# A delta-rule attention and two MoEs on one core: x^T of the first tile completed in PSUM, and the second MoE's second layer turned round

## The chip, the core and the metric

The kernel runs on one core of a Trainium2 chip. Its engines each have a queue of their own: TensorE (PE, with its weight loads as PEld), VectorE (DVE), ScalarE (ACT), GpSimd (POOL) and SyncE (SP, which here only issues DMAs). The metric is the device time of one execution in microseconds. Three runs of the kernel before took 1483.88, 1479.08 and 1480.54 us, median 1480.54. The profiled execution is another run.

## The reference

All inputs are float32 but for the first MoE's weights, which come in as 64-bit floats and are made float32 on the chip. Three stages follow each other:

```
attention, 4 batches x 8 heads, 768 steps, head size 48:
    k = k / (|k| + 1e-6)
    y[t] = q[t] . state                       # the state before this step
    state += beta[t] * k[t] (v[t] - k[t] . state)
x = y, heads side by side                     # 3072 tokens x 384
first MoE:   h = x @ w_in (384 x 2048);  x = (h * sigmoid(1.702 h)) @ w_out
second MoE:  p = domain_probs / (sum over 4 experts + 1e-9)
             out = sum over e of p[:, e] * (relu(x @ w1[e] (384 x 1024)) @ w2[e])
```

## The kernel before

**Units and tiles.** The 768 steps are cut into 12 units of 64 steps, for all batches and heads at once. Two units are one tile of 512 tokens (128 for each of the four batches), so there are 6 tiles. In a unit the recurrence is solved by blocks: a gram of the keys (`gp`, L511 and L514), the inverse of a triangular matrix (`queue_first_inverse` for units 0 and 1, on DVE with two groups of products on PE, L661 and L670; `queue_inverse` for later pairs, on POOL), a gram of queries with keys that DVE masks (the q gram, L444, L449), and then the chain (`queue_chain`): `ks`, `solve`, `cross`, `solve` again (L733, L743, L753), `read` (y, L765), `write` (L770) and the addition to the state `SU` (L784, L787). A chain is done for two halves of the heads, `hu` 0 and 1; in units 0 and 1 one half after the other.

**The way from y to x^T.** `read` leaves y in the PSUM bank with the tag `yg`, 48 rows for even heads at 0 and for odd heads at 64. `y_copy` (L773) puts three of each four heads into the tile `stage` and the fourth into another buffer; six DMAs for a unit (`put`, L848; in units 0 and 1 three on SP and three on ACT's queue) bring the fourth heads, 16 rows at a time, under the others, so that `stage` holds x^T with 128 rows in each of three blocks. Then `split_x` (L876) splits it into two float32r parts, a high one (a cast) and a low one (a subtraction, L878). Each product in the MoEs is three matmuls: high x high, high x low, low x high (`PASSES`).

**The MoEs.** For each of 16 blocks of 128 hidden columns (8 blocks in each expert of the second MoE) a visit has a first layer, 9 matmuls into `ph` (L884), and the second layer of the block before, so that the gate on ACT and DVE has a visit's time. In the first MoE the second layer has the weights stationary and 512 tokens moving, 9 matmuls into `px` (L972), and leaves x^T again. In the second MoE it has the hidden values `hh` stationary, 128 tokens at a time, and the weights moving, 12 matmuls of 384 columns into four banks `po` (L1086); rows are tokens then, and DVE multiplies by p as a scalar of each row (L1092, L1094). Each of the four experts goes over the six tiles. In tile 0 of the first MoE the first 8 blocks are done for unit 0's 256 columns, then for unit 1's, then the last 8 for 512 columns; tile 1 is done in halves throughout (`HALVED`).

**The order.** Each engine works through its own queue in the order in which the program issues. Attention and the preparation of the weights (`queue_w1`: loads, three steps that make float32 of 64-bit values, a high cast L274 and a low subtraction L277) are tasks of the planner `Order`: each has an engine or two to choose from, a cost, a priority, what it depends on, and `can`, a function that tells from when a buffer is free or None. Between the MoE's matmuls `tick` issues what is ready by the planner's clock; `until` issues tasks until the ones named are done by that clock. Before the first matmul of the first MoE stands `until(ydone[0], wdone[0])`, then one for the split.

**The second MoE's buffers.** Its weights come through `raw`, two halves of 768 columns, and are split by ACT and DVE (`split_w2`, L229 and L230); those of the next expert during the last tile. x of tiles 0 to 3 goes out to DRAM and comes back at the end of tile 4. `split_now` (L1074) splits a tile's x; that of the first tile stands behind the first MoE's end. When the first MoE ends its PSUM pools are closed (`ph` banks 0 and 1, `px` 2 to 4, the attention's `yg`, `ch0`, `ch1` 5 to 7), and the second MoE's pool takes the banks anew.

Of the kernel before, what the change touches and what calls it, by code (L numbers as in the profile page):

```python
# [149 lines left out]
def delta_attention_moe_moe_kernel(  # L150
# [17 lines left out]
    E = probs.shape[1]  # L168
    F2 = we.shape[0] // E
# [52 lines left out]

    def load_w2(n):
        nc.sync.dma_start(out=raw[:, n % 2, :], in_=we[n])

    def split_w2(n):
        t = wp.tile([128, 2, 768], F32R, name="w", tag="w")
        half = raw[:, n % 2, :]
# [94 lines left out]
    V = nc.vector  # L323

# [98 lines left out]
    def queue_q(u):  # L423
# [11 lines left out]
        for g0 in range(0, NP, 8):  # L435
# [251 lines left out]
    def queue_chain(u):  # L687
# [27 lines left out]
        for hu in range(2):  # L715
# [65 lines left out]
            def s_add(x, gs=gs, cell=cell):  # L781
# [4 lines left out]
                else:  # L786
# [3 lines left out]
                               read=read, write=write, y_copy=y_copy, s_add=s_add))  # L790


        for hs in [halves[0:1], halves[1:2]] if u < 2 else [halves]:
# [29 lines left out]
            if n == 1:  # L823
                h, = hs
                reads = [task(h["read"], "PE", 1.0, (*bs, pdone[u]), prio=p, can=lambda: free_at("yg"))]
# [4 lines left out]
            for h, y in zip(hs, reads):  # L830
                ye = h["cell"]["yev"] = [task(lambda e, x=x, h=h: h["y_copy"](e, x), ("ACT", "DVE"), (0.7, 0.72), (y,), prio=p,
                                              can=y_free) for x in range(2)]
                wr = task(h["write"], "PE", 0.82, bs, prio=p) if n == 1 else reads[0]
# [7 lines left out]


        ov = []
        for x in range(2):
            for kk in range(KD):
                def put(x=x, kk=kk):
                    d, n = DR[x] + 16 * kk, DR[x] + D
                    (nc.scalar if u < 2 and x else nc.sync).dma_start(out=xst[n:n + 16, kk, u % 2], in_=YS[u][d:d + 16])  # L848

                ov.append(task(put, "ACT" if u < 2 and x else "HW", 0.45, yev, lat=2.3, prio=p, slack=5))  # L850
# [5 lines left out]
    xst = stage.rearrange("p (k c b i) -> p k c b i", k=KD, b=B, c=2)  # L856

# [31 lines left out]
    with tc.manual_schedule():  # L889
# [6 lines left out]
        nc.gpsimd.memset(SU, 0.0)  # L896
        m2 = scr[2][:, 0:C]
# [33 lines left out]
        x1 = {}  # L931
        x1d = [drx.tile([128, KD, TT], F32, name=f"x1d{t}") for t in range(KEEP)]
# [4 lines left out]
        def queue_w2(n):  # L937
            e, f = divmod(n, F2)
            WE[e, f] = split_w2(n)
            if n + 2 < E * F2:  # L940
                load_w2(n + 2)

        def x1_out(t):
# [16 lines left out]
            return ev  # L960

# [44 lines left out]
        def split_stage(t, cs, us, fs):  # L1006
            if not us:
                return split
            until(*(ydone[u] for u in us))
            if cs.start == 0:  # L1010
# [173 lines left out]
```

## Time and profile before

| | |
|---|---|
| runs, median (lowest, highest) | 1480.54 us (1479.08, 1483.88) |
| the profiled execution | 1484.33 us |
| its span, from first to last instruction | 1482.6 us |
| mean granted TensorE clock | 0.974 of full speed |
| PE busy | 1420.4 us, 96% |
| DVE, ACT, POOL busy | 619.3, 459.8, 191.9 us |
| matmuls ph, po, px | 2808, 2304, 1080 |

The page cuts the span into 40 slices of 37 us. PE's busy tenths are 3, 6, 8, 7 in the first four and 9 from the fifth on; the granted clock is 8, 5, 8, 8 tenths in the first four and 9 or more behind them. Busy time is a union of records, and matmuls are pipelined: what a matmul costs is read from the distance of starts, not from its own duration. In the rows below the first column is the start in us from the span's start, the second the time from the first start to the last end of a merged row; a bracket at the end tells how long the engine was idle before and what ended that.

### The profile page before, as it was taken

How to read it: one execution, taken by the hardware profiler on the slowest of the kernel's cores; microseconds unless marked ns; L12 is line 12 of the kernel's file. 1: busy time of each engine (PE TensorE's matmuls, PEld its weight loads, DVE VectorE, ACT ScalarE, POOL GpSimd, SP SyncE). 2: the span in 40 equal slices, each digit the busy share in tenths (PEclk: the TensorE clock that was granted, in tenths of full speed). 3: DMA queues.
4: the chain of work that ended last, by engine and by line, in shares of the span. 5: the costliest groups of instructions: out<-in, count | busy, mean ns of one | idle time of the engine just before them, and what ended most of it. 6: DMA issues, size and time to landing. Idle time of an engine off the chain costs nothing.

```text
span 1482.6 us, 30388 instructions
## 1 busy us (share of the span) xinstructions
PE 1420.4 (96%) x13552; PEld 1258.2 (85%) x13552; DVE 619.3 (42%) x1033; ACT 459.8 (31%) x866; POOL 191.9 (13%) x340
## 2 busy tenths in 40 slices
PE   3687999999999999999999999999999999999999
PEld 2677889998888788888999999999999999999998
DVE  6978756545473423332223242232433223423222
ACT  5554434445353233432111231121321112222111
POOL 2019550080260530000000000000000000000000
PEclk8588999999999999999999999999999999999999
DMA  9211021201201000410000020000200000100001
GB/s 316 115 27 36 2 74 34 62 22 26 49 23 37 15 33 8 142 52 1 0 1 0 10 77 0 1 0 1 64 22 0 1 0 22 43 22 22 22 22 43
DMA packets 41331, 53.71 MB, mean 36 GB/s; under 512 B 25712, under 2 KB 29936, under 8 KB 41200
## 3 DMA queue, kind: packets, MB, share of 16 engines
q1 hardware_dynamic: 41008, 51.67, 11.7%
q8 instruction: 106, 1.74, 0.5%
q14 instruction: 25, 0.20, 0.0%
q10 hardware_dynamic: 192, 0.10, 0.0%
HBM read 42.71 MB, written 7.86 MB: 34 GB/s over the span
## 4 chain that ended last, share of the span: by engine, by line
PE 90%; DVE 2%; DMA 1%; ACT 1%; SPq 0%; issue 0%; DVEq 0%
PE ph L884 40%; PE po L1086 27%; PE px L972 13%; PE ch L743 2%; PE gp L444 2%; PE ch L733 1%; PE y L765 1%; DMA pq<-in_q_dram 1%; PE ch L753 1%; PE ch L770 1%; PE gp L511 1%; SPq L848 0%; DVE w L277 0%; DVE gh L990 0%; DVE scr L479 0%
## 5 line engine op out<-in xcount | busy, mean ns | idle before, releaser
L884 PE MATMUL ph<-xs,w 128*128 128x512 f32 (+1 forms) x2808 | 664.8, 379 | 3.7 <-DVE x L180 2.4
L884 PEld LDWEIGHTS ph<-xs,w 128*128 128x128 f32 x2808 | 499.7, 190 | 90.3 <-issue 2.8
L1086 PE MATMUL po<-w,hh 128*128 128x384 f32 x2304 | 432.8, 336 | 0.0
L1086 PEld LDWEIGHTS po<-w,hh 128*128 128x128 f32 x2304 | 407.6, 188 | 17.1
L1113 DVE SCALAR_TENSOR_TENSOR hh<-ph,hh 128x512 fp32r<-128x512 f32 x192 | 132.9, 692 | 554.0 <-ACT hh L1112 554.0
L1112 ACT ACTIVATE hh<-ph 128x512 fp32r<-128x512 f32 x192 | 115.0, 599 | 632.3 <-PE ph L884 632.3
L972 PE MATMUL px<-gh,w 128*128 128x512 f32 (+1 forms) x1080 | 233.5, 356 | 0.6 <-DVE gh L990 0.4
L972 PEld LDWEIGHTS px<-gh,w 128*128 128x128 f32 x1080 | 178.5, 192 | 29.4 <-DVE gh L990 2.0
L990 DVE TENSOR_TENSOR gh<-ph,gh 128x512 fp32r<-128x512 f32 (+1 forms) x120 | 69.5, 579 | 147.7 <-ACT gh L989 146.9
L987 ACT ACTIVATE ph<-ph 128x512 f32<-128x512 f32 (+1 forms) x120 | 59.5, 496 | 207.8 <-PE ph L884 203.5
L569 POOL TENSOR_TENSOR scr<-scr,itmp 128x30 f32<-128x30 f32 (+9 forms) x150 | 89.4, 596 | 11.8
L567 POOL TENSOR_TENSOR itmp<-scr 128x30 f32<-128x30 f32 (+9 forms) x150 | 81.4, 543 | 11.4
L989 ACT CAST gh<-ph 128x512 fp32r<-128x512 f32 (+1 forms) x120 | 60.2, 502 | 3.8
L180 ACT COPY su<-ch 32x384 f32<-32x384 f32 x77 | 36.2, 471 | 49.6 <-PE ch L743 45.0
L444 PE MATMUL gp<-pq,kt 48*64 48x64 f32 x768 | 34.2, 254 | 18.1 <-DMA pq<-in_q_dram 9.5
L444 PEld LDWEIGHTS gp<-pq,kt 48*64 48x64 f32 x768 | 31.3, 166 | 21.4 <-issue 8.3
L1078 DVE TENSOR_TENSOR xs<-x,xs 128x512 fp32r<-128x512 f32 x72 | 45.3, 684 | 2.0 <-ACT xs L1077 2.0
L511 PE MATMUL gp<-kt 48*32 48x64 f32 x768 | 28.2, 231 | 17.0 <-ACT kt L180 16.2
L743 PEld LDWEIGHTS ch<-v,scr 32*32 32x32 f32 x1536 | 36.5, 110 | 7.8 <-issue 4.6
L511 PEld LDWEIGHTS gp<-kt 48*32 48x32 f32 x768 | 25.2, 116 | 20.8 <-ACT kt L180 17.6
L743 PE MATMUL ch<-v,scr 32*32 32x48 f32 x1536 | 40.4, 208 | 0.7 <-DVE pq L449 0.5
L180 ACT COPY kt<-scr 32x512 f32<-32x512 f32 (+1 forms) x60 | 37.0, 617 | 12.0 <-DVE scr L333 11.1
(106 smaller groups left out, 809.6 us busy)
## 6 DMA issues: line engine op xcount, KB each, us to landing
raw<-in_we_dram SPq DMA_DIRECT2D x32, 384.0 KB, 3.1
rw<-in_w_dram SPq DMA_DIRECT2D x14, 768.0 KB, 12.2
k<-in_k_dram SPq DMA_DIRECT2D x12, 384.0 KB, 5.1
pq<-in_q_dram SPq DMA_DIRECT2D x24, 192.0 KB, 4.5
v<-in_v_dram SPq DMA_DIRECT2D x12, 384.0 KB, 3.2
out_dram<-oacc SPq DMA_DIRECT2D x24, 192.0 KB, 1.9
x1d<-raw SPq DMA_DIRECT2D x12, 256.0 KB, 2.3
x<-x1d SPq DMA_DIRECT2D x4, 768.0 KB, 5.8
```

The source lines that it names most:

```text
L180: (nc.scalar.copy if e == "ACT" else nc.vector.tensor_copy)(out=out_, in_=in_)
L444: mm(ps[TR[x]:TR[x] + C, i, :], lhsT=kt[d:d + D, g, :], rhs=pq[d:d + D, g, x, :], start=True, stop=True)
L511: mm(ps[r:r + SB, i, :], lhsT=kt[d:d + D, g, 0:SB], rhs=kt[d:d + D, g, :], start=True, stop=True)
L567: E.tensor_tensor(out=tv, in0=x[:, j:j + 1, j + 1:].broadcast_to([128, m, r]), in1=x[:, 0:m, j:j + 1].broadcast_to([128, m, r]), op=ALU.mult)
L569: E.tensor_tensor(out=x[:, 0:m, j + 1:], in0=x[:, 0:m, j + 1:], in1=tv, op=ALU.add)
L743: mm(cell["ps"][r:r + 32, i, :], lhsT=Tb[u][r:r + 32, g, :], rhs=V2[u][r:r + 32, g, :], start=True, stop=True, tile_position=(r, r))
L884: mm(ps, lhsT=w[:, a, kk * 128:(kk + 1) * 128], rhs=xs[kk][:, b, cs], start=kk == 0 and i == 0, stop=kk == KD - 1 and i == 2)
L972: mm(px[d][:, cs], lhsT=w[:, a, 384 + d * 128:384 + (d + 1) * 128], rhs=gh[:, b, 0:cs.stop - cs.start], start=f == 0 and i == 0 and cs.sta ...
L990: a = task(lambda: nc.vector.tensor_tensor(out=lo, in0=ph, in1=hi.bitcast(F32), op=ALU.subtract), "DVE", 0.07 + 0.53 * c, (a,), **kw)
L1086: mm(po[b], lhsT=hh[:, a, b * 128:(b + 1) * 128], rhs=w[:, c, 384:768], start=f == 0 and i == 0, stop=f == F2 - 1 and i == 2)
L1112: nc.scalar.activation(out=hh[:, 0, :], in_=ph, func=AF.Relu)
L1113: nc.vector.scalar_tensor_tensor(out=hh[:, 1, :], in0=ph, scalar=0.0, in1=hh[:, 0, :].bitcast(F32), op0=ALU.max, op1=ALU.subtract)
```

## The change

**x^T of the first tile.** For units 0 and 1 the rows of the fourth heads are no longer moved by DMA. A tile `S4`, which lies in `stage`'s memory and is set to zero at the start, takes from the state the columns of the fourth heads, 16 for each of three blocks, behind 48 columns of zeros (`fourth`). For each head of the first three in four, `read` now does two matmuls: one with `S4` (64 columns stationary) and the fourth head's queries, one with the head's own state on top of it. The bank then holds x^T with 64 rows in each half, and `take_x` and `take_rest` split it straight from PSUM into `xs0`. `stage`, the DMAs and `split_x` stay for the other tiles. A `can` keeps q grams of units over 1 out until the first MoE runs, and `write` in the first units now comes behind `read`.

**The second MoE.** For tiles 0 to 4 the second layer has the weights stationary and `hh` moving, 9 matmuls of 512 columns into three banks; the result has d_model in rows, so p is loaded as a row that stands in all 128 partitions (`load_pb`, into `raw`'s second half, from the DRAM tile `prd`), DVE multiplies (the first expert straight into the sum, the others in the bank and then an addition), and after the last expert DVE transposes 32x32 blocks and 16 DMAs a tile write the output. Tile 5 keeps the old form (`layer2_last`). The weights of w2 are laid out with their columns permuted to fit. The pool of `po` is opened first (banks 0 to 5), that of `ph2` second (6 and 7). The first tile's split stands at block 12 of the first MoE's last tile. The next expert's weights are split two in each of tiles 1 to 4 through `raw`'s first half.

On PE, around the first tile's first matmul (`ph`): `y` is `read`, `ch<-su,k` is `write`, `gp<-scr` the inverse's two products for unit 1, `gp<-kt_76` unit 2's gram, `gp<-pq_78,kt_76` unit 2's q gram. Before:

```order
L765 MATMUL y<-pq_78,su 48x64 x16
L770 MATMUL ch_652<-su,k_0_81 48x48 x16
L770 MATMUL ch_675<-su,k_0_81 48x48 x16
L661 MATMUL gp<-scr_100,scr_99 32x16 x64
L670 MATMUL gp<-scr_98,scr_100 32x16 x64
L765 MATMUL y<-pq_78,su 48x64 x16
...
L444 MATMUL gp<-pq_78,kt_76 64x64 x32
L884 MATMUL ph<-xs,w 128x256 x18
```

After, where `stage` is the name of `S4`'s memory:

```order
L776 MATMUL y<-pq_78,stage 64x64
L777 MATMUL y<-pq_78,su 48x64
L799 MATMUL ch_679<-su,k_0_81 48x48 x16
...
L521 MATMUL gp<-kt_76 32x32 x2
L931 MATMUL ph<-xs,w 128x256 x18
L518 MATMUL gp<-kt_76 32x64 x2
```

The inverse's products, the q gram and half of the gram have moved behind the first 18 `ph`.

On DVE, from the same place: `rw` and `w` are steps on the weights of the first MoE, `su<-ch` the state's first values, `kt` keys, `scr<-gmask,bt` the premask of units 2 and 3. Before, x^T is split (L878) 18 rows behind the last of these:

```order
L269 SCALAR_TENSOR_TENSOR rw<-rw 128x768
L787 COPY su<-ch_652 48x8x48 x2
L265 TENSOR_SCALAR rw<-rw 128x768
L269 SCALAR_TENSOR_TENSOR rw<-rw 128x768
L180 COPY kt_76<-scr_101 16x16x32
L265 TENSOR_SCALAR rw<-rw 128x768
L479 TENSOR_TENSOR scr_101<-gmask,bt 128x1024
```

After:

```order
L273 SCALAR_TENSOR_TENSOR rw<-rw 128x768
L269 TENSOR_SCALAR rw<-rw 128x768
L793 TENSOR_TENSOR xs<-y,xs 128x128 x3
L816 COPY su<-ch_656 48x8x48 x2
L273 SCALAR_TENSOR_TENSOR rw<-rw 128x768
L181 COPY kt_76<-scr_101 16x16x32
L269 TENSOR_SCALAR rw<-rw 128x768
L486 TENSOR_TENSOR scr_101<-gmask,bt 128x1024
L793 TENSOR_TENSOR xs<-y,xs 128x128 x3
L816 COPY su<-ch_679 48x8x48 x2
```

The rows are the same ones, with the state's copy (L787, now L816) two rows later; the six subtractions (L793) stand among them.

On DVE at the end of a tile in the last expert, where `hh` is the low half of the next block. Before:

```order
L1113 SCALAR_TENSOR_TENSOR hh<-ph_10295,hh 128x512
L1094 SCALAR_TENSOR_TENSOR oacc<-po,pr,oacc 128x384 x4
L1113 SCALAR_TENSOR_TENSOR hh<-ph_10324,hh 128x512
```

After:

```order
L1218 SCALAR_TENSOR_TENSOR hh<-ph_12836,hh 128x512
L1165 TENSOR_TENSOR po<-po,raw 128x512
L1166 TENSOR_TENSOR oacc_7904<-oacc_7904,po 128x16x32
L1165 TENSOR_TENSOR po<-po,raw 128x512
L1166 TENSOR_TENSOR oacc_7904<-oacc_7904,po 128x16x32
L1165 TENSOR_TENSOR po<-po,raw 128x512
L1166 TENSOR_TENSOR oacc_7904<-oacc_7904,po 128x16x32
L1171 STREAM_TRANSPOSE oacc_7904<-oacc_7904 128x768 x2
L1218 SCALAR_TENSOR_TENSOR hh<-ph_12882,hh 128x512
```

Eight operations stand between two `hh` where four stood. The diff, cut to its core:

```diff
+    xs0 = [xsp.tile([128, 2, TT], F32R, name="xs", tag="xs") for _ in range(KD)]
...
-                         (*placed[u], lq, begun[0], *ends[-1:]), prio=p + 1, can=lambda: some_free(BANKS, whole))
+                         (*placed[u], lq, begun[0], *ends[-1:]), prio=p + 1,
+                         can=lambda: None if u > 1 and not od.moe else some_free(BANKS, whole))
...
                     o, c0 = DR[x], (g * 2 + x) * D
-                    mm(py[o:o + D, i, :], lhsT=SU[:, c0:c0 + D], rhs=pq[:, g, x, :], start=True, stop=True)
+                    if not t and g % 4 == KD:
+                        continue
+                    if not t:
+                        g3 = g - g % 4 + KD
+                        mm(py[o:o + C, i, :], lhsT=S4[:, g // 4, x, g % 4, :], rhs=pq[:, g3, x, :], start=True, stop=False)
+                    mm(py[o:o + D, i, :], lhsT=SU[:, c0:c0 + D], rhs=pq[:, g, x, :], start=bool(t), stop=True)
+
+            def fourth(e, hu=hu):
+                bs = slice(hu * B // 2, (hu + 1) * B // 2)
+                copy(e, S4[:, bs, :, :, D:].rearrange("p b x k i -> p (b x k) i"),
+                     SU[:, 0:NP * 2 * D].rearrange("p (b m y) -> p b m y", b=B, m=4)[:, bs, KD, :])
+
+            def take_x(e, kk, hu=hu, cell=cell):
+                c0 = (u % 2) * TT // 2 + hu * TT // 4
+                copy(e, xs0[kk][:, 0, c0:c0 + TT // 4].rearrange("p (b i) -> p b i", i=C),
+                     cell["py"].rearrange("p (b m) i -> p m b i", m=4)[:, kk])
...
+                bs.append(task(h["fourth"], ("ACT", "DVE"), (0.35, 0.35), bs, prio=p))
+                reads = [task(h["read"], "PE", 1.5, (*bs, pdone[u]), prio=p, can=lambda: free_at("yg"))]
...
+                    for kk in range(KD):
+                        a = task(lambda e, kk=kk, h=h: h["take_x"](e, kk), ("ACT", "DVE"), (0.3, 0.27), (y,), prio=-2)
+                        ye += [a, task(lambda kk=kk, h=h: h["take_rest"](kk), "DVE", 0.28, (a,), prio=-2)]
...
+        if not t:
+            direct[u] = yev
+            ydone[u] = task(lambda: None, None, 0.0, yev, lat=0.0, prio=p)
+            return
...
+    S4 = stage.rearrange("p (b x k i) -> p b x k i", b=B, x=2, k=KD)
...
         nc.gpsimd.memset(SU, 0.0)
+        nc.gpsimd.memset(stage, 0.0)
...
+                if t == NW - 1 and f == F1 - 4:
+                    first = [split_now(0, 0, kk) for kk in range(KD)]
...
+        pso = ctx.enter_context(tc.tile_pool(name="pso", bufs=6, space=PSUM))
         ps2 = ctx.enter_context(tc.tile_pool(name="ps2", bufs=2, space=PSUM))
...
+            pb[e, t] = raw[:, 1, 0:TT]
+            nc.sync.dma_start(out=pb[e, t], in_=prd[e:e + 1, t * TT:(t + 1) * TT].broadcast_to([128, TT]))
...
         def layer2_2(e, t, f, hh, w):
+            acc = oacc[t].rearrange("p (c k j) -> p k c j", k=KD, j=32)
+            for kk in range(KD):
+                if f == 0:
+                    po[kk] = pso.tile([128, TT], F32, name="po", tag="po")
+                for i, (a, c) in enumerate(PASSES):
+                    mm(po[kk], lhsT=w[:, a, 384 + kk * 128:384 + (kk + 1) * 128], rhs=hh[:, c, :],
+                       start=f == 0 and i == 0, stop=f == F2 - 1 and i == 2)
+                if f == F2 - 1:
+                    ps = po[kk]
+                    if e == 0:
+                        nc.vector.tensor_tensor(out=acc[:, kk], in0=ps.rearrange("p (c j) -> p c j", j=32),
+                                                in1=pb[e, t].rearrange("p (c j) -> p c j", j=32), op=ALU.mult)
+                        continue
+                    nc.vector.tensor_tensor(out=ps, in0=ps, in1=pb[e, t], op=ALU.mult)
+                    nc.vector.tensor_tensor(out=acc[:, kk], in0=acc[:, kk], in1=ps.rearrange("p (c j) -> p c j", j=32),
+                                            op=ALU.add)
+            if f == F2 - 1 and e == E - 1:
+                for h in range(2):
+                    half = oacc[t][:, h * KD * TT // 2:(h + 1) * KD * TT // 2]
+                    nc.vector.transpose(out=half, in_=half)
...
+                if e + 1 < E and 1 <= t <= F2 // 2 and f in (2, 4):
+                    queue_w2((e + 1) * F2 + (t - 1) * 2 + f // 2 - 1)
...
-        layer2_2(*pend)
+        (layer2_last if pend[1] == NW - 1 else layer2_2)(*pend)
```

## Rows read from the trace of the kernel before

**Rows 1.** The page: busy us, share of the span and instructions of each engine.

```profile
PE 1420.4 (96%) x13552; PEld 1258.2 (85%) x13552; DVE 619.3 (42%) x1033; ACT 459.8 (31%) x866; POOL 191.9 (13%) x340
```

**Rows 2.** Timeline of PE from 66 to 91 us: start, us, line, what.

```profile
66.61 1.54 PE L661 MATMUL gp<-scr,scr 32*32 32x16 f32 x128 [1.61 <-DVE su L787]
69.87 1.90 PE L670 MATMUL gp<-scr,scr 32*32 32x16 f32 x128 [1.71 <-ACT scr L180]
71.70 1.95 PE L765 MATMUL y<-pq,su 128*48 128x64 f32 x32
...
82.94 3.67 PE L444 MATMUL gp<-pq,kt 48*64 48x64 f32 x62 [0.86 <-DMA pq<-in_q_dram]
86.55 4.21 PE L884 MATMUL ph<-xs,w 128*128 128x256 f32 x18
```

**Rows 3.** Windows, 25 to 75 us: length, then each engine's busy time, clock, DMA.

```profile
25.00:75.00 50.00, 30.77 (x1059) 28.52 (x1058) 43.61 (x90) 28.03 (x45) 0.00 (x0) 0.56 0.47 186
```

**Rows 4.** Timeline of PE from 118 to 154 us.

```profile
118.56 1.10 PE L765 MATMUL y<-pq,su 128*48 128x64 f32 x32
...
131.55 2.29 PE L884 MATMUL ph<-xs,w 128*128 128x256 f32 x9
...
151.75 2.23 PE L884 MATMUL ph<-xs,w 128*128 128x512 f32 x9
```

**Rows 5.** Timeline of DVE from 61 to 83 us.

```profile
61.08 1.82 DVE L417 TENSOR_TENSOR k<-k,scr 128x768 f32<-128x768 f32 x2
...
63.30 1.30 DVE L333 STREAM_TRANSPOSE scr<-k 128x512 f32<-128x512 f32 x2
...
68.99 1.22 DVE L479 TENSOR_TENSOR scr<-gmask,bt 128x1024 f32<-128x1024 f32 x1
...
82.45 0.42 DVE L878 TENSOR_TENSOR xs<-stage,xs 128x256 fp32r<-128x256 f32 x1 [0.46 <-ACT xs L180]
```

**Rows 6.** Timeline of DVE from 130 to 133 us.

```profile
130.65 1.00 DVE L265 TENSOR_SCALAR rw<-rw 128x768 int32<-128x768 int32 x1
131.69 1.25 DVE L269 SCALAR_TENSOR_TENSOR rw<-rw 128x768 int32<-128x768 int32 x1
```

**Rows 7.** Timeline of PE from 189 to 206 us.

```profile
189.46 1.64 PE L770 MATMUL ch<-su,k 64*48 64x48 f32 x64
...
193.76 1.10 PE L765 MATMUL y<-pq,su 128*48 128x64 f32 x32
...
197.28 2.07 PE L733 MATMUL ch<-su,kt 48*64 48x48 f32 x64
...
205.17 1.34 PE L884 MATMUL ph<-xs,w 128*128 128x256 f32 x9
```

**Rows 8.** Timeline of PE from 640 to 680 us, end of the first MoE.

```profile
641.01 2.20 PE L972 MATMUL px<-gh,w 128*128 128x512 f32 x9
...
669.57 4.29 PE L972 MATMUL px<-gh,w 128*128 128x512 f32 x18
676.30 4.36 PE L884 MATMUL ph<-xs,w 128*128 128x512 f32 x18 [2.43 <-DVE x L180]
```

**Rows 9.** The chain that ended last, in the second MoE: start, us, what.

```profile
684.85 2.10 PE po L1086 x12
...
1370.39 2.10 PE po L1086 x12
```

**Rows 10.** Timeline of DVE from 911 to 917 us, at a tile's end.

```profile
911.28 0.69 DVE L1113 SCALAR_TENSOR_TENSOR hh<-ph,hh 128x512 fp32r<-128x512 f32 x1 [3.50 <-ACT hh L1112]
...
915.46 0.69 DVE L1113 SCALAR_TENSOR_TENSOR hh<-ph,hh 128x512 fp32r<-128x512 f32 x1 [1.38 <-ACT hh L1112]
```

**Rows 11.** Timeline of PE at the same tile's end.

```profile
918.80 2.24 PE L1086 MATMUL po<-w,hh 128*128 128x384 f32 x12
```

**Rows 12.** Timeline of POOL, inverse of units 2 and 3.

```profile
104.55 0.16 POOL L561 MEMSET scr<- 128x32 f32 x1 [94.20 <-PE ph L884]
...
153.83 1.92 POOL L573 TENSOR_TENSOR scr<-scr,bt 128x1024 f32<-128x1024 f32 x1
```

More of the change, by code (lines that the diff above doesn't have):

```diff
@@ L789, in queue_chain @@
             halves.append(dict(hu=hu, cell=cell, ks=ks, rest=rest, solve=solve, solved=solved, cross=cross, rest2=rest2,
-                               read=read, write=write, y_copy=y_copy, s_add=s_add))
+                               read=read, write=write, y_copy=y_copy, s_add=s_add, fourth=fourth,
+                               take_x=take_x, take_rest=take_rest))
         for hs in [halves[0:1], halves[1:2]] if u < 2 else [halves]:
@@ L830, in queue_chain @@
             for h, y in zip(hs, reads):
-                ye = h["cell"]["yev"] = [task(lambda e, x=x, h=h: h["y_copy"](e, x), ("ACT", "DVE"), (0.7, 0.72), (y,), prio=p,
-                                              can=y_free) for x in range(2)]
-                wr = task(h["write"], "PE", 0.82, bs, prio=p) if n == 1 else reads[0]
+                if t:
+                    ye = [task(lambda e, x=x, h=h: h["y_copy"](e, x), ("ACT", "DVE"), (0.7, 0.72), (y,), prio=p,
+                               can=y_free) for x in range(2)]
+                else:
+                    ye = []
+                    for kk in range(KD):
+                        a = task(lambda e, kk=kk, h=h: h["take_x"](e, kk), ("ACT", "DVE"), (0.3, 0.27), (y,), prio=-2)
+                        ye += [a, task(lambda kk=kk, h=h: h["take_rest"](kk), "DVE", 0.28, (a,), prio=-2)]
+                    xfree.setdefault((0, 0), []).append(y)
+                    xfree.setdefault((0, 1), []).append(y)
+                h["cell"]["yev"] = ye
+                wr = task(h["write"], "PE", 0.82, (y,), prio=p) if n == 1 else reads[0]
                 se = [task(lambda x=x, h=h: h["s_add"](x), "DVE", 0.47, (wr, y), prio=p) for x in range(2)]
@@ L847, in put @@
                     d, n = DR[x] + 16 * kk, DR[x] + D
-                    (nc.scalar if u < 2 and x else nc.sync).dma_start(out=xst[n:n + 16, kk, u % 2], in_=YS[u][d:d + 16])
-                ov.append(task(put, "ACT" if u < 2 and x else "HW", 0.45, yev, lat=2.3, prio=p, slack=5))
+                    nc.sync.dma_start(out=xst[n:n + 16, kk, u % 2], in_=YS[u][d:d + 16])
+                ov.append(task(put, "HW", 0.45, yev, lat=2.3, prio=p, slack=5))
         whole["end"] = ov
@@ L960, in x1_out, with split_now @@
             return ev
+        def split_now(n, t, kk):
+            s = (xsp if n % 2 else xs2).tile([128, 2, TT], F32R, name="xs", tag="xs")
+            src = x1[t][:, kk, :]
+            nc.scalar.copy(out=s[:, 0, :], in_=src)
+            nc.vector.tensor_tensor(out=s[:, 1, :], in0=src, in1=s[:, 0, :].bitcast(F32), op=ALU.subtract)
+            return s
         evac = []
@@ L1009, in split_stage @@
             until(*(ydone[u] for u in us))
+            if not t:
+                xs[:] = xs0
+                return [a for u in us for a in direct[u]]
             if cs.start == 0:
@@ L1064, in delta_attention_moe_moe_kernel @@
                 load_w2(1)
[L1065 removed]
+                nc.sync.dma_start(out=pr, in_=probs)
         layer2_1(*pend)
@@ L1097, in layer2_2 @@
                         r0 = b * S + t * 128
-                        nc.sync.dma_start(out=out[r0:r0 + 128, :], in_=acc)
+                        nc.sync.dma_start(out=out[r0:r0 + 128, :], in_=acc[:, b])
         pend = None
         seq = [(e, t) for e in range(E) for t in range(NW)]
-        xs = [split_now(0, 0, kk) for kk in range(KD)]
+        load_pb(0)
+        pr5 = big.tile([128, E, B], F32, name="pr5")
+        for e in range(E):
+            nc.sync.dma_start(out=pr5[:, e], in_=prd[e, (NW - 1) * TT:].rearrange("(b p) -> p b", b=B))
+        xs = first
         for n, (e, t) in enumerate(seq):
```

81 lines of the change are left out of this document (51 added, 30 removed).

## The prediction

> **What bounds the kernel now.** I read the page first. PE is busy for 96% of the span [rows 1], so only two things can move the time: stretches in which PE does not work or works slowly, and the time that a matmul takes where PE never stops. The page's slices of PE and of its clock put the first kind into the first tenth of the span and show the second everywhere behind it. So I read three stretches in the timeline: the start up to the first tile's first matmul, the pure stretch of the first MoE beside the second MoE, and the seam between them.
>
> At the start PE waits for x^T of unit 0. Its second half of y is done at 71.70 + 1.95 = 73.65 us, but the first ph comes at 86.55 [rows 2]. In between stand the DMAs that bring the fourth heads into `stage`, the split, and 64 matmuls for unit 2's q (the last 62 take 3.67 us) which the planner put there because it thought PE free. DVE sets the pace before: it is busy for 43.6 of the 50 us from 25 to 75 [rows 3]. The same picture comes back for unit 1: y is done at 118.56 + 1.10 = 119.66, and ph goes on at 131.55 [rows 4], with a group of q matmuls between.
>
> **First tile, unit 0.** Until 61.08 us DVE's order is the same row for row. From there to the premask (the 128x1024 product with gmask) it keeps the same twelve instructions, which took from 61.08 to 68.99 + 1.22 = 70.21, 9.1 us without a gap [rows 5]; six subtractions of 128x128 now stand among and behind them. One of 128x256 takes 0.42, so these cost between 0.2 and 0.42; I take 0.3. So x^T of unit 0 is ready at 61.08 + 9.1 + 1.8 = 72.0, where PE started on it at 86.55. What ACT and PE add lies beside DVE: the copy of the fourth heads, three casts a half, 24 matmuls a half for 16. The second half's y must wait until the first half has left the bank `yg`: that lies within the walk, since five rows of DVE stand between the two groups of subtractions.
>
> **Unit 1.** What is moved behind the first ph is unit 1's two inverse products (1.54 and 1.90, [rows 2]), half a gram of unit 2 (about 1) and unit 2's q matmuls, all on a PE that until then idled. Before, PE went without a gap from 86.55 to 119.66, 33.1 us. Now this stretch takes 33.1 + 3.4 + 1 + 2 (the q matmuls at the higher clock, about half of 3.67) + 1.1 (half as many y matmuls again) = 40.6, from 72 to 112.6; with the last casts and subtractions unit 1's x^T is there at 114. DVE, walked in the same way through the W blocks, comes out at 114 too: the two are level, and I expect small waits on both. Before, it was 131.55: some 17 us are won here.
>
> **The pass over unit 1** ran from 131.55 to 151.75, 20.2 us [rows 4]. Now DVE has more left to do in it: three more W blocks want their tensor_scalar and their shift, 1.00 and 1.25 while POOL works beside [rows 6], 6.8 us together, of which its gaps take some; unit 3's q matmuls lie in it too, about 2. I take 23: the first 512-wide ph at 137 instead of 151.75, 14 us won.
>
> **The seam to tile 1** gives some back. Unit 2's x^T still goes through `stage` and the DMAs, and in the new order nothing but attention stands between unit 2's y and tile 1's first ph. From the second y's end to that ph it took 205.17 - 194.86 = 10.3 us [rows 7], some 8 of it chain; with two reads of 1.1 and a copy of about 1 between them the chain from the first y is 11.3 us, in which PE has two reads 2.2, the write 1.64, ks 2.07 and a solve of some 1.5, 7.5 us of work. So 3.8 us idle, which were none. Left: 10.5 us. Behind it PE is full to 673 us in either order but for single microseconds, so a start that is earlier by so much ends earlier by as much. Bounds: 3 us (a seam of 8, W blocks late as well) and 17 (nothing given back).
>
> **Costed at nothing.** The memset of `stage` on POOL moves PQ[1]'s and with it q's second load and all behind it on SP, by one memset (between 1 and 2 us by its size). DVE's own chain of the first inverse, up to 40 us, hides that; without the cover it is those 1 to 2 us. Six DMAs on SP instead of three there and three on ACT matter for no tile: the first two units now issue none, and from tile 1 on all six were SP's already.
>
> **Seam of the MoEs.** Before, PE is idle for 2.43 us up to 676.30, released by DVE's last copy of px [rows 8]. Now the first split is made four blocks earlier, and the first two ph2 lie in banks 6 and 7, whose last users were the chains, long done; px's banks are wanted two ph2 later, 4 us. So 2.5 us go (bounds 0 and 2.6, the gap that a stream without a stop would leave).
>
> **Second MoE, second layer turned.** A visit is 9 matmuls of 512 columns for the first layer and, for five of six tiles, now 9 of 512 instead of 12 of 384: 4608 columns both ways. So the price of a matmul beyond its columns decides. Before: from the po at 684.85 to the one at 1370.39 there are 164 visits, 4.180 us each [rows 9]. The first MoE's pure stretch has the new form already (the weights stationary in both layers, 512 columns): from 641.01 to 669.57 stand seven visits, 4.080 us each [rows 8]. The difference, 0.100 us by 160 visits, is 16.0 us. The bound on the other side is the ph group of the second MoE itself: 4.18 - 2.10 = 2.08 where the first MoE has 2.04. Were the turned group to take 2.08 too, 3 us would be won; if it kept 2.10, nothing. I take 16, because the first MoE has both shapes and the unevenness can come only from the mixture of 512 and 384, which goes away.
>
> The Trainium skill speaks against this: its page "TensorE: Matmul & The Clock Gate", section "Back-to-back issue gap", gives N / 2.4 + 2.5 ns for one matmul behind another at the full clock. By that page 9 x 215.8 stand against 12 x 162.5 ns, 8 ns a visit, and turning the layer round would win 1 us in all. The trace disagrees with it: 126 matmuls of 512 in 28.56 us are 226.7 ns each [rows 8].
>
> On DVE each tile's end costs more: a multiplication in the bank and an addition for each of three blocks from the second expert on, six of 512 for four of 384; in the last expert two transposes of 128x768 more (128x512 takes 0.65 to 0.70 in [rows 5], so about 1.0 each). Queued behind them is the next block's hh. Before, one hh starts at 911.28 and the next at 915.46, and the second lasts to 916.15 [rows 10], so 3.5 us lie between; six operations at hh's 0.69 take 4.1, with transposes 6.1. PE reads that hh in the po group at 918.80 [rows 11], 2.7 us later, so a delay of 0.6 or 2.6 is just covered. If it isn't, the five transposing tiles lose up to 1 us each. The split of the weights, spread over four tiles instead of packed into one, finds 3.5 us free in a visit. The load of p has six visits to land in.
>
> **Sum.** 10.5 + 2.5 + 16 = 29 us off the profiled execution's 1484.3 make 1455.3. That execution stands 3.8 over the median of the runs, 1480.5, so the median becomes 1451.5; I say 1452.
>
> **Rivals.**
> - The turned layer wins nothing: a matmul of 512 goes on costing what it costs in the second MoE now. For it: ph takes 2.08 there. Against: the first MoE runs the same two shapes at 2.04. Then 13 us are won: 1467. Chance 0.14.
> - The start is given back: POOL's inverse for units 2 and 3 began at 104.55 and ended at 155.75 [rows 12], and by my walk it begins no earlier now. Unit 2's chain can't start before 158; it would start at 167, so POOL has 9 us of room. If unit 3's grams come later by more, the start keeps 4 us: 1458. Chance 0.13.
> - Slower: DVE at the ends of tiles. It decides from the point at which six operations take over 3.5 + 2.7 = 6.2 us, 1.03 each. To eat 29 us over the 15 ends that have six, each must lose 2 us more, 1.4 an operation, and then 5 us more for a slower kernel: 1486. Rows that are twice what their size asks stand in the trace only beside POOL, which rests by then. Chance 0.03.
> - The start gives all it can (17): 1445. Chance 0.06. The first two together: 1474, 0.02.
>
> The forecast itself, 1445 to 1459, has 0.62. Outside 1442 to 1467 I leave some 0.15: the slower case, the double one, half of the first. A difference of under 0.3% (4.4 us) can't be told from none. Faster: 0.62 + 0.14 + 0.13 + 0.06 - 0.01 = 0.94; same 0.03; slower 0.03.
>
> **What will show it.** The first 256-wide ph at 71 to 75 us, the second half's at 112 to 118, the first 512-wide at 135 to 141, an idle stretch of 2 to 6 us before tile 1 at 190 to 197. No wait on PE at the seam of the MoEs. Po groups of 9 in the second MoE at 2.04 us, visits of 4.08, and 4.18 still in each expert's last tile. Wrong would be: visits over 4.15, a PE wait for DVE behind each tile's end, or an idle PE of over 8 us at tile 1.

## The result

| | before | after |
|---|---|---|
| runs, median (lowest, highest), 9 runs each on one chip | 1481.11 us (1477.26, 1484.11) | 1467.61 us (1465.33, 1478.28) |
| the profiled execution | 1484.33 us | 1465.33 us |
| its span | 1482.6 us | 1463.6 us |
| mean granted TensorE clock of that execution | 0.974 | 0.992 |

The ratio is 0.9917, with an interval from 0.9895 to 0.9938: 0.8% faster. The forecast was 1452; the time stands just above the range's end of 1467. It is the number of the first rival ("the turned layer wins nothing", 1467), but the trace below shows that this is not what happened: in two tiles of six the layer won all that was forecast.

Between the two profiled executions there are 19.0 us. They divide so: the last px of the first MoE comes 9.9 us earlier, the seam between the MoEs gives 2.6 and the second MoE 6.3; the last 0.2 lie behind the last matmul. The rise of the mean clock is no measure of the gain: most of it lies between 26 and 64 us, where the execution before stood at 0.50 while DVE set the pace. The run e6_start_only, below, stood at 0.50 there too, and its DVE came to the first row of [rows 5] at 59.98 us, against 59.41 after and 61.08 before.

### The profile page after: what moved, and what is told of

It is laid out like the page before. It is cut to its first block, busy times and chain, and to the rows that moved or that the text cites. A ratio compares the mean times of both kernels' runs of the same rounds, so it can differ in the third digit from the quotient of the medians.

```text
span 1463.6 us, 29678 instructions
## 1 busy us (share of the span) xinstructions
PE 1414.7 (97%) x13136; PEld 1196.0 (82%) x13136; DVE 647.8 (44%) x1067; ACT 457.4 (31%) x867; POOL 191.5 (13%) x341
## 4 chain that ended last, share of the span: by engine, by line
PE 91%; DVE 3%; issue 1%; DMA 1%; ACT 0%; SPq 0%; DVEq 0%
PE ph L931 40%; PE po L1157 23%; PE px L1029 13%; PE po L1187 5%; PE ch L750 2%; PE y L777 2%; PE ch L740 1%; PE ch L760 1%; PE ch L799 1%; PE gp L518 1%; PE gp L450 1%; DVE w L281 0%; DMA pq<-in_q_dram 0%; DVE pq L455 0%; DVE gh L1047 0%
## 5 line engine op out<-in xcount | busy, mean ns | idle before, releaser
L1157 PE MATMUL po<-hh,w 128*128 128x512 f32 x1440 | 355.9, 391 | 0.0
L1157 PEld LDWEIGHTS po<-hh,w 128*128 128x128 f32 x1440 | 270.4, 188 | 60.4
L1187 PE MATMUL po<-w,hh 128*128 128x384 f32 x384 | 73.9, 342 | 0.0
L1187 PEld LDWEIGHTS po<-w,hh 128*128 128x128 f32 x384 | 69.3, 188 | 2.5
```

What stands on the lines that cost most here:

```text
L1157: mm(po[kk], lhsT=w[:, a, 384 + kk * 128:384 + (kk + 1) * 128], rhs=hh[:, c, :], start=f == 0 and i == 0, stop=f == F2 - 1 and i == 2)
L1187: mm(ps, lhsT=hh[:, a, b * 128:(b + 1) * 128], rhs=w[:, c, 384:768].rearrange("p (k a i) -> p a k i", a=4, k=KD), start=f == 0 and i == 0, ...
```

## The profile after

First the page: busy time by engine, and the granted clock in 40 slices of 37 us.

```profile
PE 1414.7 (97%) x13136; PEld 1196.0 (82%) x13136; DVE 647.8 (44%) x1067; ACT 457.4 (31%) x867; POOL 191.5 (13%) x341
PEclk9999979999999999999999999999999999999999
```

Against [rows 1] PE has 416 matmuls fewer: 480 by the turned layer (3 in each of 160 visits), and 64 more for the first tile's x^T. One slice of the clock is at 7, the sixth.

The start, in PE's timeline (start us, length, line, what), against [rows 2, 4]:

```profile
69.96 2.42 PE L931 MATMUL ph<-xs,w 128*128 128x256 f32 x18
...
113.03 1.55 PE L931 MATMUL ph<-xs,w 128*128 128x256 f32 x9
...
134.25 2.23 PE L931 MATMUL ph<-xs,w 128*128 128x512 f32 x9
```

The three checkpoints came 16.6, 18.5 and 17.5 us earlier than before. On DVE the two rows between which the prediction walked, the first of its twelve instructions and the last three subtractions:

```profile
59.41 1.83 DVE L423 TENSOR_TENSOR k<-k,scr 128x768 f32<-128x768 f32 x2
...
69.16 0.69 DVE L793 TENSOR_TENSOR xs<-y,xs 128x128 fp32r<-128x128 f32 x3
```

Then the seam to tile 1, where [rows 7] had no rest at all:

```profile
177.13 1.66 PE L1029 MATMUL px<-gh,w 128*128 128x512 f32 x6
178.72 1.55 PE L750 MATMUL ch<-v,scr 32*32 32x48 f32 x64
...
184.97 1.14 PE L740 MATMUL ch<-su,kt 48*64 48x48 f32 x32
187.69 1.21 PE L740 MATMUL ch<-su,kt 48*64 48x48 f32 x32 [1.59 <-DVE su L813]
188.84 2.77 PE L750 MATMUL ch<-v,scr 32*32 32x48 f32 x64
191.53 0.58 PE L931 MATMUL ph<-xs,w 128*128 128x256 f32 x1
192.90 2.08 PE L931 MATMUL ph<-xs,w 128*128 128x256 f32 x8 [0.79 <-DVE xs L925]
...
197.60 2.93 PE L1029 MATMUL px<-gh,w 128*128 128x512 f32 x6
```

PE waits 1.59 us for DVE's addition to the state and 0.79 for the split of x^T. The solve of 64 matmuls behind the first wait takes 2.77 us where the one in tile 0 at 178.72 took 1.55, and the six px at 197.60 take 2.93 where those at 177.13 took 1.66: the clock has gone down. The windows of this stretch for the kernel after and the kernel before (length; busy time and count of PE, PEld, DVE, ACT, POOL; then clock, share of the DMA engines, GB/s):

```profile
192.00:206.00 14.00, 13.21 (x153) 11.19 (x152) 4.39 (x8) 5.73 (x12) 6.06 (x12) 0.51 0.34 83
```

```profile
192.00:206.00 14.00, 14.00 (x260) 11.42 (x260) 7.51 (x17) 4.68 (x10) 12.12 (x25) 1.00 0.34 69
```

PE is busy for 13.21 of the 14 us at a clock of 0.51, where it was 1.00 before. (The counts of 153 and 260 can't be set against each other, since the two windows hold other matmuls.) Call lead the time by which the n-th matmul of ph and px starts earlier than in the kernel before: it was 17.5 us at the 300th and is 5.3 at the 720th. Some 3.3 come back between the 1440th and the 1560th, and they belong to the execution of before: there PE waited once for q (the waits of before from 485 to 505 us: total, times, longest), and behind that its clock was at 0.57 from 497 to 501 us.

```profile
PE gp L444 <- DMA pq<-in_q_dram: 1.5, 1, 1.5
```

The seam between the MoEs, against [rows 8]: no wait stands ahead of the two ph2.

```profile
659.64 4.30 PE L1029 MATMUL px<-gh,w 128*128 128x512 f32 x18
663.77 4.36 PE L931 MATMUL ph<-xs,w 128*128 128x512 f32 x18
667.97 2.23 PE L1157 MATMUL po<-hh,w 128*128 128x512 f32 x9
```

The second MoE, in an odd tile (1), an even tile (2) and tile 5 of the first expert. Read the distances of the starts:

```profile
711.44 2.20 PE L931 MATMUL ph<-xs,w 128*128 128x512 f32 x9
713.48 2.20 PE L1157 MATMUL po<-hh,w 128*128 128x512 f32 x9
715.52 2.20 PE L931 MATMUL ph<-xs,w 128*128 128x512 f32 x9
...
744.48 2.26 PE L931 MATMUL ph<-xs,w 128*128 128x512 f32 x9
746.58 2.24 PE L1157 MATMUL po<-hh,w 128*128 128x512 f32 x9
748.66 2.26 PE L931 MATMUL ph<-xs,w 128*128 128x512 f32 x9
...
841.78 2.31 PE L1187 MATMUL po<-w,hh 128*128 128x384 f32 x12
843.94 2.20 PE L931 MATMUL ph<-xs,w 128*128 128x512 f32 x9
845.98 2.31 PE L1187 MATMUL po<-w,hh 128*128 128x384 f32 x12
```

A visit lasts 4.08 us in tiles 1 and 3, as forecast; 4.18 in tiles 0, 2 and 4; 4.19 in tile 5 (2.15 for its po, 2.04 for ph). PE waits for nobody in the second MoE: no wait of PE from 667 us to the end stands in the profile, at the tiles' ends either. The clock is 1.00 in all these tiles.

## The experiments

Two questions: why do three of the five turned tiles keep the old price, and where does the start's lead go? What differs between odd and even tiles is the pool of x^T: odd tiles read `xsp`, even tiles `xs2`. The two pools lie in different places. Counting in bytes within a partition of SBUF, the weights, `xsp` and hh all begin 160 bytes past a multiple of 2048; `xs2` stands behind three small tiles of 544 bytes and begins 704 past one.

**The place of xs2.** Edit:

```diff
+ small = ctx.enter_context(tc.tile_pool(name="small", bufs=1))   # behind xs2
- pr = big.tile(...); ptmp = big.tile(...); pr5 = big.tile(...)
+ pr = small.tile(...); ptmp = small.tile(...); pr5 = small.tile(...)
```

> The changed kernel, with the three x^T tiles of the pool xs2 moved in SBUF: they stand in front of pr, ptmp and pr5 (544 bytes) instead of behind them, so they begin at byte 215200 of a partition and not at 215744. Nothing else moves. Why: in the changed kernel a visit of the second MoE lasts 4.08 us in tiles 1 and 3 and 4.18 us in tiles 0, 2 and 4. Tiles 1 and 3 read x^T from the pool xsp, whose tiles begin, like the weights and hh, 160 bytes past a multiple of 2048; the even tiles read it from xs2, 704 bytes past one. Theory 'place': a matmul of 512 costs 226.7 ns or 231 to 233 ns by where its moving tile lies against the others. Then all five turned tiles take 4.08 a visit, tile 5 keeps 4.20, and the whole is 96 visits x 0.10 = 9.6 us less, less what the ends of tiles already have: 7 to 10 us under the changed kernel, about 1459. Theory 'parity': the even tiles are slow because their output stands in other PSUM banks than that of the odd tiles, or because of what DVE and ACT do in them. Then the even tiles keep 4.18 and the time stays at 1467.

Measured: 1458.47 us, ratio to before 0.9847 (0.9823 to 0.9871), with six executions from 1454.78 to 1477.67; the spread is a matter of the start, below. Tile 2 in its timeline, where 4.18 stood:

```profile
746.73 2.20 PE L931 MATMUL ph<-xs,w 128*128 128x512 f32 x9
748.77 2.20 PE L1158 MATMUL po<-hh,w 128*128 128x512 f32 x9
750.81 2.20 PE L931 MATMUL ph<-xs,w 128*128 128x512 f32 x9
```

All five turned tiles take 4.080; tile 5 takes 4.193. "Place" holds, "parity" falls.

**The same move in the kernel before.** The edit is that of e1_place, for pr and ptmp.

> The kernel before, with xs2 moved in the same way (in front of pr and ptmp, 480 bytes earlier). There the odd tiles read xs2 and take 4.173 us a visit, the even ones read xsp and take 4.187. Theory 'place': it is the only cause of unevenness, so the odd tiles fall to 2.04 + 2.08 = 4.12 (9 matmuls of 226.7 and 12 of 173.3 ns) and 96 visits win 5 us; the even tiles stay. Theory 'mixture' (the prediction's): 512 and 384 columns side by side make matmuls uneven wherever the tiles lie. Then the odd tiles become like the even ones, 4.187, and the time is the same or 1 us longer.

Measured: 1482.51, ratio 1.0009 (0.9998 to 1.0020). Tile 2:

```profile
745.72 2.24 PE L884 MATMUL ph<-xs,w 128*128 128x512 f32 x9
747.80 2.27 PE L1087 MATMUL po<-w,hh 128*128 128x384 f32 x12
749.91 2.24 PE L884 MATMUL ph<-xs,w 128*128 128x512 f32 x9
```

Every tile takes 4.187, the odd ones too, which had 4.173. So the forecast of "mixture", the prediction's reason, comes out as well: with the old second layer the place gains nothing. Whether it is the 384 columns beside 512 isn't shown: the old layer also has `hh` stationary and the weights moving, and no run changes only one of the two. By themselves such groups are even; the last two of the kernel before, with no ph between or behind them:

```profile
1474.71 4.33 PE L1086 MATMUL po<-w,hh 128*128 128x384 f32 x24
```

The last twelve of these start every 173 or 174 ns, 2.08 us for a group; in e4_before_place a group beside ph takes 2.11. The layer has to be turned and xs2 to be moved; each alone leaves tiles of the second MoE uneven, and both together bring 4.187 down to 4.080 in the turned tiles.

**How far apart.** Three pads on the changed kernel, and one that moves all tiles together and keeps their distances:

```diff
- ptmp = big.tile([128, NP_], ...)
+ ptmp = big.tile([128, NP_ + n], ...)[:, 0:NP_]      # n = 8 (e2_plus32), 24 (e10_128), 56 (e11_256)
- raw = const.tile([128, 2, 768], ...)                # e3_all32: 32 bytes more ahead of everything
+ raw = const.tile([128, 2 * 768 + 8], ...)[:, 0:2 * 768].rearrange(...)
```

> The changed kernel with xs2 moved by 32 bytes (ptmp is padded): its tiles begin at 215776, which is 32 past a multiple of 64 as the weights, hh and xsp are, but 736 past a multiple of 2048 where those are 160 past one (64 off them modulo 512). Theory 'within 64 bytes': what counts is where in 64 bytes a moving tile begins against the others; then all turned tiles take 4.08 us a visit. Theory 'wider': what counts is the place modulo 512 or 2048; then the even tiles keep 4.16 to 4.18, or take some third value.

> The changed kernel with everything behind raw moved by 32 bytes (raw is padded): weights, xsp and hh now begin at a multiple of 64 and xs2 32 past one, so the distances between them are those of the changed kernel. Theory 'distance': the place against the other tiles counts; then the even tiles take 4.18 us a visit as before and the odd ones and the first MoE 4.08. Theory 'place itself': a moving tile that begins at a multiple of 64 is slow; then the odd tiles and the first MoE's pure stretch become slow, and the even tiles' ph fast.

> The changed kernel with xs2 128 bytes past where the other tiles stand, modulo 512 (ptmp is padded by 96 bytes). Distances so far: 0 gives visits of 4.08, 32 gives 4.18, 64 gives 4.147. If the distance has to be a multiple of 512, the even tiles are uneven again, with a value of their own, above 4.08; if of 128, they take 4.08.

> As the run e10_128, with xs2 256 bytes past the others modulo 512. If the distance has to be a multiple of 512, the even tiles take more than 4.08 a visit; if of 256 or less, 4.08.

Tile 2 in the timelines of e2_plus32, e3_all32, e10_128 and e11_256, in this order:

```profile
747.61 2.22 PE L931 MATMUL ph<-xs,w 128*128 128x512 f32 x9
749.67 2.25 PE L1157 MATMUL po<-hh,w 128*128 128x512 f32 x9
751.76 1.54 PE L931 MATMUL ph<-xs,w 128*128 128x512 f32 x6
```

```profile
747.27 2.26 PE L931 MATMUL ph<-xs,w 128*128 128x512 f32 x9
749.37 2.24 PE L1157 MATMUL po<-hh,w 128*128 128x512 f32 x9
```

```profile
745.88 2.26 PE L931 MATMUL ph<-xs,w 128*128 128x512 f32 x9
747.97 2.23 PE L1157 MATMUL po<-hh,w 128*128 128x512 f32 x9
750.04 2.26 PE L931 MATMUL ph<-xs,w 128*128 128x512 f32 x9
```

```profile
746.74 2.20 PE L931 MATMUL ph<-xs,w 128*128 128x512 f32 x9
748.78 2.20 PE L1157 MATMUL po<-hh,w 128*128 128x512 f32 x9
750.82 2.20 PE L931 MATMUL ph<-xs,w 128*128 128x512 f32 x9
```

| xs2's distance to the others, modulo 512 bytes | 0 | 32 | 32, all moved by 32 | 64 | 128 | 256 |
|---|---|---|---|---|---|---|
| visit of tile 2, us | 4.08 | 4.18 | 4.18 | 4.15 | 4.16 | 4.08 |

The odd tiles keep 4.08 in all of them. It is the distance that counts, not the place itself, and of the distances tried 0 and 256 are even. Neither "within 64 bytes" nor the multiple of 512 holds. Weights, `xsp` and hh never moved against each other, so which of them x^T has to keep the distance to isn't shown. (Each of the four is one execution; their whole times, 1474.31, 1468.10, 1481.66 and 1459.44, differ by these visits and, by up to 15 us at the last px, by the start, which comes further down.)

**Tile 5.** Its second layer reads the weights' columns in runs of 32. Edit, on e1_place:

```diff
- rhs=w[:, c, 384:768].rearrange("p (k a i) -> p a k i", a=4, k=KD)
+ rhs=w[:, c, 384:768]          # the last addition on DVE puts the columns in order, in 4 pieces
```

> The kernel of the run e1_place; in tile 5 the second layer reads its 384 weight columns in the order in which they lie, one run of 1536 bytes, and not as 12 runs of 128 bytes; DVE puts the columns in order with its last addition, in four pieces for each block of tokens. In e1_place a po group of tile 5 lasts 2.15 us, 12 matmuls of 180 ns, and ph beside it 2.04. Theory 'runs': the runs cost the 7 ns; then 12 x 173.3 = 2.08, visits of 4.12, 32 x 0.073 = 2.3 us less, less about 1 us for smaller additions at the end. Theory 'mixture': 512 and 384 columns side by side make matmuls uneven when both stream without a stop, as the 4.187 us a visit of the kernel before with xs2 moved suggest; then visits take 4.187, and nothing is won.

```profile
850.77 2.24 PE L931 MATMUL ph<-xs,w 128*128 128x512 f32 x9
852.85 2.27 PE L1188 MATMUL po<-w,hh 128*128 128x384 f32 x12
854.96 2.24 PE L931 MATMUL ph<-xs,w 128*128 128x512 f32 x9
```

4.187 a visit for 4.193: "mixture" again, with the same reservation. Its four executions (median 1469.40, ratio 0.9888, 0.9829 to 0.9948) spread too far for such a difference; the trace decides.

**Each part alone.** The second MoE's hunks of the diff on the kernel before, and the first tile's:

> The kernel before with the second MoE's part of the change alone (the layer turned round, its banks, the early split and the probabilities); the first tile's x^T still goes through stage. By the trace of the changed kernel: the seam of the MoEs gives 2.6 us, the second MoE 6.3 (3 matmuls fewer a visit at 13.3 ns each, 160 visits = 6.4). So 9 us under the kernel before, 1472. By the prediction: 2.5 + 16 = 18.5 us, 1462.

> The kernel before with the first tile's part alone: x^T of units 0 and 1 completed in PSUM; the second MoE as before. By the prediction 10.5 us are won, 1470.5. By the trace of the changed kernel, where the lead of 17 us at the first 512-wide ph is 6 us behind the seam to tile 1 (PE idles there and its clock falls to 0.50 from 189 to 205 us): 6 us, 1475. If a wait for q's DMA at 495 us, which only the profiled execution before had (3.4 us with the clock's fall), is part of most executions of the kernel before, 9.5 us, 1471.5.

The second MoE alone: 1474.11, ratio 0.9949 (0.9937 to 0.9961), 8 us for 9 expected by the trace and 18.5 by the prediction. The start alone: 1483.17, ratio 1.0009 (0.9984 to 1.0034), nothing at all, so all three expected times were missed. Its twelve executions ran from 1475.54 to 1496.93, while all 23 of the kernel before lay between 1478.62 and 1486.64. In its profiled execution, and in that of e1_place, the lead is lost in two places: at the seam to tile 1, and already from 84 us on. There PE rests in the middle of the 128 small matmuls of unit 1's second inverse product, and no releaser is named. This row is the rest in e1_place, the next is the changed kernel's:

```profile
84.56 0.87 PE L677 MATMUL gp<-scr,scr 32*32 32x16 f32 x82 [1.41 <-issue]
```

```profile
83.02 0.86 PE L677 MATMUL gp<-scr,scr 32*32 32x16 f32 x82 [0.75 <-issue]
```

And the windows behind it, e1_place first, then the changed kernel: in the same order of matmuls, 353 at a clock of 0.56 against 583 at 1.00.

```profile
84.00:106.00 22.00, 21.43 (x353) 19.45 (x353) 10.16 (x18) 7.51 (x17) 0.00 (x0) 0.56 0.01 2
```

```profile
84.00:106.00 22.00, 22.00 (x583) 19.98 (x584) 18.70 (x32) 13.54 (x30) 2.55 (x8) 1.00 0.05 9
```

So the profiled execution of the changed kernel was a lucky one in its first 110 us. Of the nine profiled executions that have the new start and no added matmuls, six lost the clock there for 20 us and more.

**PE kept at work.** Matmuls whose results nobody uses, in the places where PE rests, on e1_place:

```diff
+ def keep_busy(ps, n):
+     for _ in range(n):
+         mm(ps[:, 0:256], lhsT=W[0][:, 0, 0:128], rhs=W[0][:, 1, 0:256], start=True, stop=True)
  # e7_seam_filled: 12 ahead of the second half of unit 3's ks, 14 ahead of tile 1's first ph
  # e9_both_filled: also 8 ahead of unit 1's second inverse product
```

> The kernel of the run e1_place with 26 matmuls more, of 256 columns, which compute nothing that is used: 12 between the two halves of unit 3's ks and 14 ahead of tile 1's first ph, in the bank of that ph. They stand where PE waits at the seam from tile 0 to tile 1 (1.59 us for DVE's additions to the state, 1.4 us and less for the split of x^T). In three executions of kernels with the new start the granted clock falls to 0.50 some 1 to 3 us behind the first of these waits and stays there for 16 us. Theory 'clock': the fall follows from PE's rest, so with PE at work there it doesn't come; the 16 us at 0.50 hold some 14 us of work that takes 7 at 1.0, so about 7 us go: 1451 against 1458. Theory 'chain': DVE's and ACT's chain sets the pace behind the seam, PE at half its clock is just as long as that; then the clock stays up and the time stays within 2 us of 1458. Theory 'other': the fall comes from elsewhere and comes all the same.

> The kernel of the run e7_seam_filled with 8 more matmuls of 256 columns that compute nothing that is used, ahead of unit 1's second inverse product (0.96 us of work). There PE rests in the middle of the 128 small matmuls, and the profile names no releaser for it: 0.75 us in the changed kernel's profiled execution, 0.99 to 1.41 us in four others. Where the rest was 0.75 the granted clock stayed at 1.0; behind 0.99 it fell for 4 us and behind 1.15 to 1.41 for 17 to 20 us, in which the run loses about 9 us on the changed kernel's. Theory 'rest': the length of PE's rest decides over the fall. If the matmuls ahead of it shorten the rest below 0.9 us, the clock stays at 1.0 from 84 to 105, and the last px comes at 656 to 660 us, where e7_seam_filled had 667.7; the median falls from 1458 to about 1450. Theory 'chain': DVE sets the pace there too, or the rest moves to another place; then the last px stays between 665 and 670 and the median at 1456 to 1460.

The windows of the seam in e7_seam_filled, and the windows from 84 us in e9_both_filled:

```profile
190.00:206.00 16.00, 15.90 (x364) 14.04 (x363) 9.06 (x18) 5.86 (x15) 13.88 (x28) 1.00 0.37 86
```

```profile
84.00:106.00 22.00, 21.74 (x572) 19.65 (x572) 18.18 (x32) 13.42 (x30) 2.23 (x8) 1.00 0.03 6
```

In e7_seam_filled the clock stays up at the seam and the last px comes 7.1 us earlier than in e1_place, 0.8 of which it had ahead of the seam, as "clock" expects. But its early rest was 1.15 us and its clock from 84 to 106 us 0.53, and the median, 1458.15 (ratio 0.9823, 0.9797 to 0.9849), can't be told from e1_place's. I expected 1451: missed. With both places filled the rest shrinks to 0.32 us, the last px comes 6.6 us earlier still, and the median is 1453.84, ratio 0.9796 (0.9779 to 0.9812), with five executions within 4.2 us. I had expected 1450, and the last px 1 us sooner than it came (661.35 for 656 to 660).

**The start alone, with PE kept at work.** The 34 matmuls on e6_start_only:

> The kernel of the run e6_start_only (the first tile's part of the change alone, the second MoE as before) with the 34 matmuls of e9_both_filled that keep PE at work in its rests before unit 1's second inverse product and at the seam to tile 1. They cost 4 us of PE's work, most of it in time in which PE rested. Theory 'clock': what ate the prediction's 10.5 us for the start is the granted clock, which falls to 0.50 behind those rests; with them filled the last px comes at 660 to 664 us (673.5 in the kernel before), the median is 1471 to 1473 and no execution is above 1478, where e6_start_only ran from 1475.5 to 1497. Theory 'start': the new start is worth nothing by itself, and the 5 us between e1_place and e9_both_filled are of other origin; then the median stays between 1478 and 1483.

Measured: 1473.68, just above the expected range, ratio 0.9930 (0.9916 to 0.9945), executions from 1470.67 to 1474.99, the last px at 659.96, 13.5 us earlier than in the profiled execution before (which had the wait for q). With PE kept at work the new start wins 9.8 us; without, nothing. "Clock" holds. The kernel before was not run with such matmuls, so how much of the 9.8 they would give without the new start isn't shown.

## Why the prediction was wrong

By its own steps:

- **Unit 0, unit 1, the pass over unit 1: right in this execution, not in most.** Forecast 71 to 75, 112 to 118 and 135 to 141; measured 69.96, 113.03 and 134.25. Unit 0 came earlier because DVE's walk began at 59.41 and not at 61.08; the walk itself took 10.4 us for the 10.9 of the sum. But in the six executions that lost the clock from 84 us on, unit 1's ph came at 122.0 to 128.9 and the first 512-wide one at 143 to 150. The step had counted PE's work at the higher clock; a fall of the clock behind a rest it had at nothing.
- **The seam to tile 1: the place right, its size wrong.** Tile 1's first ph at 191.53 (forecast 190 to 197), idle 2.4 us (forecast 2 to 6). But the step counted idle time alone (its own numbers, 14.75 less 3.8, make 11 rather than 10.5). Behind the rest PE runs at half its full clock until about 205 us, and that is the larger loss: filling the rests gave 6.3 us at the seam. That the profiled kernel shows 9.9 us of lead in the end, close to the 10.5 of the sum, is luck: 3.3 are a wait in the execution of before, and its own first rest was short. By the runs the start is worth 0 (alone) to 4.7 us (0.9949 against 0.9917), not 10.5.
- **The seam between the MoEs: right.** 2.6 us for 2.5.
- **The second MoE: this is the step that failed most.** "I take 16, because the first MoE has both shapes and the unevenness can come only from the mixture of 512 and 384, which goes away." The old layer beside ph was one cause, whether by its 384 columns or by its operands; the distance of xs2 from the other tiles is a second, which the trace of before hid, because there all tiles were uneven. The row that could have warned was in the same trace: odd and even tiles differed by 0.013 us a visit (4.173 and 4.187), and what alternates there is the pool of x^T. The mean over 164 visits [rows 9] had it averaged away. 96 visits went from 4.187 to 4.180, 64 from 4.173 to 4.080, and tile 5's 32 became dearer by 0.02 (4.193 for 4.173), where I had said they would keep 4.18: 6.3 us in all. With xs2 moved the term is 96 x 0.107 + 64 x 0.093 = 16 us, what the step had said.
- **Of the 0.107 of an even tile, the count of matmuls is the smaller part.** An even matmul costs 226.7 ns at 512 columns and 173.3 at 384. The difference is 0.417 ns a column, a column a cycle of 2.4 GHz; so the columns make 213.3 and 160.0, 13.3 ns come on top of either, and three matmuls fewer save 0.040 us a visit. The other 0.067 are unevenness. The Trainium skill's page "TensorE: Matmul & The Clock Gate", section "Back-to-back issue gap", gives 2.5 ns on top, for a matmul taken by itself, and some 131 ns at 512 columns for a stream of matmuls with their weight loads; these rows, where every matmul has a weight load, agree with neither.
- **DVE at the tiles' ends, the split, the load of p: right,** all covered; the slower rival had no part in it.
- **The executions.** I set the profiled execution 3.8 us above the median and took that off. The one of after stands 2.3 below its own median. That is 6 us of the 15.6 between forecast and result; 9.6 are the second MoE. By medians it reads otherwise: the second MoE with its seam gave 8.0 us for 18.5 (e5_second_only), and the start 0 to 4.7 for 10.5. The two accounts differ because the profiled execution after had a good start and the one before a wait for q.

The version with both conditions restored, e9_both_filled, takes 28.2 us off the kernel before, where the sum said 29. So the gains could be had; by the medians the uneven distance took some 9 us of them (1467.61 to 1458.47) and the clock some 5 (to 1453.84).

## What to carry to other kernels

Where PE never stops, look at the start-to-start distances of single matmuls per tile: if equal instructions differ, compare where their tiles lie in SBUF, and keep small odd-sized tiles behind the large ones, so that moving tiles and weights lie 0 or 256 bytes apart modulo 512, the two distances that were even here. A change that takes work out of PE's early, loose stretch is to be priced with the clock behind each new rest, not by idle time; and one execution of such a start says little, so count several before a few microseconds are believed.

## What the runs showed of the hardware

- Matmuls of 512 columns start every 226.7 ns when the moving tiles and the weights lie 0 or 256 bytes apart modulo 512, and every 229 to 233 ns on the mean when they lie 32, 64 or 128 apart. The unevenness spreads: in the even tiles of the changed kernel the po groups take 2.08 instead of 2.04 although their own tiles, hh and weights, lie as in the odd ones. All this is at a clock of 1.00 and with a weight load for every matmul. The Trainium skill's page "SBUF — State Buffer", section "SBUF: two separate sides", says that PE never waits on anyone at its ports. The runs show that PE's pace depends on where its operands lie; whether the reads of the weights and of the moving tile get into each other's way, as I suppose, no run here shows.
- Groups of 384 columns, with hh stationary, between groups of 512 were uneven, and the 512s with them (4.187 us in e4_before_place and e8_last_straight at distance 0, in the kernel before 4.187 at distance 0 and 4.173 at 480, in the odd tiles; 4.120 if all were even). Why is open. With the moving tile in runs of 128 bytes the 512s beside it stayed even, and the 384s took 180 ns instead.
- A rest of PE in the middle of 128 small matmuls that wait for nothing named: 0.75 to 1.43 us in the profiled executions with the new start, 0.28 and 0.32 with eight long matmuls ahead of it. What it waits for isn't shown. Behind those of 1.04 to 1.43 us (six executions) the clock was at 0.50 for 20 us and longer, behind those of 0.75, 0.99 and 1.03 not at all or for some 3 us. The length of a rest doesn't decide alone: a longer one, 2.8 to 3.0 us ahead of unit 1's second y, was followed in the same nine executions by only some 3 us at 0.50. That is what these executions did, no rule.
